# Two channels per position in the exchanged tile, and the first chunk's taps on TensorE

## The chip, the cores and the metric

The kernel runs on one NeuronCore of one Trainium2 chip. The metric is device time in microseconds (us) of one execution. All operands are float32. The engines are TensorE (PE; its weight loads are listed apart as PEld), VectorE (DVE), ScalarE (ACT), GpSimd (POOL) and SyncE (SP), which issues nearly all DMAs. Each engine takes its instructions in the order of the program.

## What is computed

The sequence has 2,048 positions, the model 512 channels. The reference, cut to what matters:

```python
# A: short causal convolution of k (4 taps per channel), times v,
#    then a causal convolution of 2,048 taps per channel, done with FFTs
k_shift = sum(k_pad[:, t:t + S, :] * shift_k[:, ks - 1 - t] for t in range(ks))
kv = k_shift * v
y = irfft(rfft(kv, 2 * S) * rfft(ssm_k, 2 * S))[:S] + kv * ssm_D
a = q * y
# B: two tokens of the 2,048 are chosen by a score and go through a SwiGLU FFN
r = x @ w_r                                  # x is q
idx = argsort(-r)[:2]
upd = (silu(x[idx] @ w_gate) * (x[idx] @ w_up)) @ w_down * sigmoid(r[idx])
b = x; b[idx] += upd
g = sigmoid((x * gate_w).sum(-1))
out = g * a + (1 - g) * b                    # = q * (g * y + (1 - g)), plus two rows
```

## The kernel before

The 512 channels are worked in four chunks of 128 (`c` = 0 to 3). The long convolution is done with Fourier transforms written as matrix products: a transform of 2,048 is split into one of 64 and one of 32, with a change of layout between them. Each chunk goes through these steps, which are named generators in the code; `c` is the chunk, the other index a part of it:

- `taps(c, x)`, x = 0 to 3: the four taps of k on a quarter of the positions, channels on partitions. ScalarE scales the first shifted window of `kT` into `acc` (line 167). For chunk 0 VectorE adds the other three (line 171, `TAPS_DVE`); for chunks 1 to 3 ScalarE scales each into `tap` (line 174) and GpSimd adds it (line 176).
- `T(c, x)`: TensorE transposes `acc` in four blocks of 128 x 128 into PSUM (line 185), and VectorE multiplies the result by v into the chunk's `kv` tile (line 187).
- `A(c, b)`, b = 0 to 3: the transform of 64 of the long filter `hN` (line 158). Before it `D(t)` (`skip`, lines 138 to 142) adds the row `drow` to the filter's first tap on GpSimd.
- `C(c, b)`: the same transform of `kv` (line 199). It needs all four T of the chunk.
- `exchange` (line 149), once for each A and each C, eight times a chunk: VectorE transposes 32 x 32 blocks of the PSUM result, 128 x 1024, into the tile `e`, where now the 32 inner positions lie on the partitions. `e` is laid out [channel group, position k, 4 channels].
- `S(c, u)`, u = 0 to 7: the transform of 32 of both, filter and kv, for four positions k each (line 212): 16 matmuls that run on tiles of 64 rows x 32 columns of the array. The moving operand is `e[r, :, k, :]`, 64 groups (two halves of 32) of 4 channels. It needs all eight exchanges of the chunk. ScalarE copies one factor out of PSUM (`g`, line 217), VectorE forms the two products of spectra (lines 222, 223), and GpSimd their sums (line 229).
- `I(c, u)`: the inverse transform of 32 (line 241), copied by ScalarE into `f` (line 246). `f` is laid out [channel pair, position, 2 channels].
- `X(c, i)`: VectorE transposes 32 x 32 blocks of `f` in place (line 254).
- `J(c, mb)`: the inverse transform of 64 (line 263), whose moving operand is `f[:, :, k, :]`, 64 groups of 2 channels; the gate g*y + (1-g) on ScalarE (line 271; on VectorE, line 273, for two blocks of the last chunk), the product with q on GpSimd (line 276; VectorE for those two), and the store.
- `G` (`ffn`): router, choice of the two tokens and FFN, cut into about thirty pieces, on TensorE with small steps on VectorE. `Z(c)` adds the update of the two rows to chunk c's output by an indirect DMA on GpSimd's queue (line 401).

Loads are steps too: `Lk` (`kT`), `Lv` (v), `Lh` (the filter), `Lq` (q), `Lw` (q transposed for the router, then the FFN's weights: the tile `wff`) take the next piece of a stream, `L0` to `L11` the constants (`w1`, `w2`, `w3`, `vv` are the transforms' matrices, `ident` the identity, `shk` the taps). All are issued on SP, in order; a load into a buffer in use waits there, and what stands behind it waits too. `kT` has two buffers of two parts each, v three buffers, `hN` and `wff` two each, q four.

The order of everything is written out by hand, in the string `ORDER`: each word advances that generator to its next `yield`, and what it issues there stands in each engine's program in that order. No planner changes it. PSUM is divided by hand as well: pool `ps2` has three buffers, used by A, C, S, I and the last chunk's J; pool `ps` has one, for T and the other J; pool `psf` one, for G.

Of the kernel before, what the change touches and what calls it, by code (L numbers as in the profile page):

```python
# [8 lines left out]
F32 = mybir.dt.float32  # L9
# [7 lines left out]
S, D, F = 2048, 512, 1792  # L17
NC, DC = 4, 128
# [5 lines left out]
TAPS_DVE = {(0, 0), (0, 1), (0, 2), (0, 3)}  # L24
# [7 lines left out]
L5 L3 Lk L0 Lk L8 taps0.0 taps0.1 taps0.0 taps0.0 Lk taps0.0 Lk Lv L2 Lv taps0.1 taps0.1 taps0.2 L1 L4 taps0.1 L9  # L32
taps0.2 Lh taps0.2 taps0.3 D0 Lw T0.1 Lh Lk Lw T0.1 taps0.3 D1 T0.0 L10 T0.0 A0.0 Lv taps0.3 taps0.3 Lv A0.1 A0.2
taps0.2 A0.2 T0.3 A0.0 Lv taps1.0 taps1.0 T0.3 G taps1.0 A0.3 Lk Lh Lk T0.2 A0.3 taps1.0 Lw Lw T0.2 Lh C0.0 A0.1
C0.0 C0.1 C0.2 C0.3 Lv Lk taps1.1 taps1.1 taps1.2 D2 L6 G C0.1 Lw taps1.1 C0.3 taps1.2 C0.2 taps1.1 taps1.2 A1.1
A1.0 A1.1 A1.0 T1.0 S0.2 taps1.3 T1.0 S0.0 Lw taps1.2 S0.2 S0.1 taps1.3 D3 Lk S0.2 T1.1 Lk G S0.0 taps1.3 S0.1 S0.0
taps1.3 S0.1 S0.1 L7 A1.2 taps2.1 S0.3 A1.2 Lv taps2.1 S0.3 Lv Lw S0.5 Lw T1.1 S0.5 I0.0 taps2.1 T1.3 G S0.5 S0.3
S0.3 S0.4 T1.3 S0.4 S0.4 I0.0 S0.6 I0.0 T1.2 Lh taps2.1 S0.5 Lq Lw T1.2 G A1.3 D4 I0.1 taps2.0 A1.3 S0.6 taps2.0 G
Lv I0.1 S0.6 C1.0 T2.1 Lv C1.0 Lk G I0.1 Lw C1.2 C1.2 C1.1 taps2.0 Lh C1.1 S0.7 taps2.2 taps2.0 taps2.2 G Lk S0.7
C1.3 C1.3 S0.7 T2.1 I0.2 A2.1 G taps2.2 taps2.2 S1.2 Lv T2.0 I0.2 I0.2 A2.1 G S0.7 I0.3 taps2.3 T2.0 taps2.3 G S1.2  # L40
T2.2 S1.0 S1.2 Lk I0.3 I0.3 S1.0 S1.0 S1.1 taps2.3 taps2.3 S1.1 S1.3 S1.1 S1.1 S1.3 G T2.2 S1.4 taps3.0 taps3.0 S1.4
S1.3 G Lk I1.0 L11 D5 S1.4 G G A2.0 Lw Lw I1.0 I1.0 taps3.1 Lv A2.3 X0.1 A2.0 T2.3 S1.3 S1.5 Lq A2.3 X0.0 S1.7 G
S1.5 Lv taps3.0 G Lq S1.5 S1.5 taps3.0 X0.3 S1.7 Lw I1.1 I1.2 Lw I1.1 I1.1 Lk T2.3 X0.2 C2.3 C2.3 S1.7 J0.0 J0.0 G
taps3.1 I1.2 G J0.0 taps3.1 Lh I1.2 taps3.1 J0.1 C2.1 A2.2 Lw Lw Lq C2.1 J0.1 C2.0 J0.1 C2.2 C2.0 A2.2 C2.2 Lh
taps3.2 G G Lk J0.2 J0.2 S1.6 S2.1 Lw Lw S2.0 J0.3 S1.6 G D6 G S1.6 taps3.2 J0.2 S2.1 S2.1 Lv A3.0 Lv Lw S2.0 S2.0
S1.7 A3.1 A3.1 J0.3 taps3.2 I1.3 T3.1 J0.0 A3.0 D7 taps3.3 Lw T3.1 taps3.2 I1.3 I1.3 S2.1 S2.3 taps3.3 Lv X1.2 S2.3
S2.2 T3.2 S2.3 T3.2 G X1.1 Lw G S2.2 A3.3 I2.0 taps3.3 taps3.3 I2.0 I2.0 T3.3 A3.3 T3.3 J0.3 S2.6 Lq S2.2 S2.7 X1.0
T3.0 S2.3 S2.7 G S2.7 Lw J0.2 G I2.1 Lw A3.2 S2.6 S2.6 T3.0 I2.1 I2.1 X1.3 S2.5 S2.5 S2.5 S2.4 J0.1 J1.2 A3.2 S2.4
S2.7 Lw G G C3.0 C3.0 I2.3 Lq S2.4 G I2.3 I2.3 C3.1 C3.3 C3.2 C3.1 C3.3 Lw S2.5 J1.2 I2.2 Lw C3.2 Lq J1.0 J0.3 J1.2
Lq I2.2 I2.2 J1.0 S3.0 S3.0 X2.0 J1.0 S3.1 S3.7 S3.1 X2.2 J1.1 S3.0 J1.1 J1.1 J1.2 S3.1 Lq X2.1 S3.7 G Lw S3.6 S3.7  # L50
S3.6 S3.6 S3.2 S3.1 S3.2 Lw J1.3 X2.3 I3.0 J1.1 S3.7 S3.2 J1.0 J1.3 Lq J1.3 S3.3 S3.3 S3.3 S3.3 G J2.2 J2.2 Lq S3.5
# [468 lines left out]
```

## Time and profile before

| | |
|---|---|
| median of 3 runs | 198.1 us (197.37 to 198.25) |
| the profiled execution | 198.09 us, of which 196.1 us are the span shown by the profile |
| TensorE busy | 146.9 us (75%) |
| TensorE weight loads busy | 70.3 us (36%) |
| VectorE busy | 150.6 us (77%) |
| ScalarE busy | 93.3 us (48%) |
| GpSimd busy | 115.4 us (59%) |
| DMA | 39.77 MB, mean 203 GB/s |

A group in the profile has the line, the engine, the operation, the output and its inputs by name, partitions x elements, and the count; then busy time in us and the mean length of one in ns; then the idle time of the engine just before these instructions and what ended it. In the order of time a row begins with its start and its length in us, and merges neighbours. A row of waits names who waited, for whom, the total in us, how many times, and the longest. A row of a window has its bounds and length, then the busy time (and count) of TensorE, its weight loads, VectorE, ScalarE and GpSimd, the granted TensorE clock, the busy share of the DMA engines, and GB/s. The trace lists each float32 matmul as two records of matmul and two of weight load; a transpose on TensorE is one.

### The profile page before, as it was taken

To read this page: it belongs to the slowest core of one execution; us is meant where nothing else is said; L and a number is where in the kernel's file an instruction comes from. 1 tells how busy PE (TensorE), PEld (TensorE's weight loads), DVE (VectorE), ACT (ScalarE), POOL (GpSimd) and SP (SyncE) were. 2 spreads that over 40 slices of the span, in tenths; PEclk is the share of its full clock that TensorE was granted. 3 is DMA by queue.
4 is the path that set the end of the run, shared out by engine and by line. 5 is a ranking of instruction groups with operands and counts; after the bars stand their busy time and mean duration, and the time that the engine had idled before them with its cause. 6 is when DMAs were issued, how large, how long until landed. Compare 5 with 4: busy or idle time off the path is not lost. (4 is left out here: it accounts for less than half of the span.)

```text
span 196.1 us, 4562 instructions
## 1 busy us (share of the span) xinstructions
PE 146.9 (75%) x1822; PEld 70.3 (36%) x1822; DVE 150.6 (77%) x179; ACT 93.3 (48%) x178; POOL 115.4 (59%) x107
## 2 busy tenths in 40 slices
PE   0028748788978797998897999899989997974700
PEld 0014222334523234542443534444356452423600
DVE  0198799997889998999769879988999845047540
ACT  0611655265597245753395672432556555660500
POOL 0021889159899276974595898460613992931662
PEclk9999999999999999999999999999999999998885
DMA  5999994858699300079578464675640757786140
GB/s 133 366 324 273 341 341 166 295 196 310 210 322 349 119 0 4 3 246 336 194 271 278 159 230 142 208 232 174 187 149 24 261 140 242 184 275 209 60 159 0
DMA packets 16473, 39.77 MB, mean 203 GB/s; under 512 B 2361, under 2 KB 2883, under 8 KB 16325
## 3 DMA queue, kind: packets, MB, share of 16 engines
q1 hardware_dynamic: 16292, 39.48, 60.7%
q8 instruction: 14, 0.23, 0.5%
q0 software_dynamic: 160, 0.01, 0.2%
q14 instruction: 7, 0.05, 0.1%
HBM read 35.28 MB, written 4.20 MB: 201 GB/s over the span
## 5 line engine op out<-in xcount | busy, mean ns | idle before, releaser
L149 DVE STREAM_TRANSPOSE e<-p 128x1024 f32<-128x1024 f32 x32 | 62.8, 2041 | 5.6 <-PE p L199 2.9
L229 POOL TENSOR_TENSOR y<-y 128x512 f32<-128x512 f32 x32 | 40.3, 1282 | 21.6 <-DVE y L222 21.3
L176 POOL TENSOR_TENSOR acc<-acc,tap 128x512 f32<-128x512 f32 x36 | 45.9, 1280 | 11.1 <-ACT tap L174 6.7
L212 PE MATMUL p<-e,w 64*32 64x256 f32 x1024 | 32.7, 380 | 5.9 <-DVE e L149 5.1
L241 PE MATMUL p<-y,w 64*128 64x512 f32 x128 | 31.8, 611 | 3.2 <-POOL y L229 1.4
L246 ACT ACTIVATE f<-p 128x512 f32<-128x512 f32 x32 | 18.1, 625 | 25.2 <-PE p L241 25.1
L276 POOL TENSOR_TENSOR qN<-oA,qN 128x512 f32<-128x512 f32 x14 | 17.9, 1278 | 20.3 <-ACT oA L271 16.2
L217 ACT ACTIVATE g<-p 128x512 f32<-128x512 f32 x32 | 18.9, 598 | 22.5 <-PE p L212 15.0
L222 DVE TENSOR_TENSOR y<-p,g 128x512 f32<-128x512 f32 x32 | 21.8, 682 | 9.3 <-PE p L241 4.1
L174 ACT ACTIVATE tap<-kT,shk 128x512 f32<-128x512 f32 x36 | 25.4, 718 | 4.3 <-POOL acc L176 4.1
L212 PEld LDWEIGHTS p<-e,w 64*32 64x32 f32 x1024 | 17.7, 106 | 19.8 <-DVE e L149 8.5
L254 DVE STREAM_TRANSPOSE f<-f 128x1024 f32<-128x1024 f32 x16 | 19.3, 1223 | 7.0 <-ACT f L246 7.0
L185 PE MATMUL ps<-ident,acc 128*128 128x128 f32 x64 | 11.4, 305 | 16.1 <-DVE acc L171 13.5
L271 ACT ACTIVATE oA<-ps,omg,gcol 128x128 f32<-128x128 f32 x48 | 18.0, 460 | 11.4 <-PE ps L263 9.1
L223 DVE TENSOR_TENSOR y<-p,g 128x512 f32<-128x512 f32 x32 | 21.8, 683 | 1.0 <-POOL y L229 0.7
L199 PE MATMUL p<-kv,w 64*128 64x512 f32 x64 | 17.3, 640 | 5.1 <-DVE e L149 2.1
L158 PE MATMUL p<-hN,w 64*128 64x512 f32 x64 | 18.0, 661 | 1.8 <-DVE e L149 1.2
L241 PEld LDWEIGHTS p<-y,w 64*128 64x128 f32 x128 | 11.5, 186 | 18.4 <-issue 9.3
L185 PEld LDWEIGHTS ps<-ident,acc 128*128 128x128 f32 x64 | 7.3, 150 | 25.6 <-DVE acc L171 13.5
L167 ACT ACTIVATE acc<-kT,shk 128x512 f32<-128x512 f32 x16 | 11.2, 719 | 10.9 <-DMA kT<-in_kT_dram 10.8
L171 DVE SCALAR_TENSOR_TENSOR acc<-kT,shk,acc 128x512 f32<-128x512 f32 x12 | 8.7, 748 | 9.1 <-ACT acc L167 8.9
L140 POOL TENSOR_TENSOR hN<-hN,drow 1x32 f32<-1x32 f32 x16 | 5.2, 324 | 15.0 <-DMA hN<-in_hN_dram 14.4
(63 smaller groups left out, 117.0 us busy)
## 6 DMA issues: line engine op xcount, KB each, us to landing
vN<-in_vN_dram SPq DMA_DIRECT2D x16, 256.0 KB, 5.2
hN<-in_hN_dram SPq DMA_DIRECT2D x8, 512.0 KB, 5.3
wff<-in_qT_dram SPq DMA_DIRECT2D x8, 512.0 KB, 5.6
qN<-in_qN_dram SPq DMA_DIRECT2D x16, 256.0 KB, 3.4
out_dram<-qN SPq DMA_DIRECT2D x16, 256.0 KB, 3.8
wff<-in_wg_dram SPq DMA_DIRECT2D x8, 448.0 KB, 4.1
wff<-in_wu_dram SPq DMA_DIRECT2D x8, 448.0 KB, 4.6
wff<-in_wd_dram SPq DMA_DIRECT2D x8, 448.0 KB, 5.6
```

Of the source, the lines that this page charges most:

```text
L149: nc.vector.transpose(ee[c][:, i, b * 8:(b + 1) * 8].rearrange("p d k e -> p d e k"), p)
L174: nc.scalar.activation(s, w[j], AF.Copy, scale=shk[:, c, j:j + 1])
L176: nc.gpsimd.tensor_add(acc, acc, s)
L185: nc.tensor.transpose(p[:, i], acc[:, i * 128:(i + 1) * 128], ident)
L212: nc.tensor.matmul(p[32 * j:32 * j + 32, b, ri].rearrange("p i d -> p (i d)"), w2[r, 4 * u + j, 32 * ri:32 * ri + 32], e[r, :, 4 * u + j, ...
L217: nc.scalar.activation(g, p[:, :, :, 0], AF.Copy)
L222: nc.vector.tensor_mul(y1[:, u % 2], p[:, :, :, 1], g)
L223: nc.vector.tensor_mul(y2[:, u % 2], p[:, :, ::-1, 1], g)
L229: nc.gpsimd.tensor_tensor(w[:, :, 0], w[:, :, 0], w[:, :, 1], op=op)
L241: nc.tensor.matmul(p[:, j], w3[r, w], y[r, :, ri], start=(n == 0), stop=(n == len(parts) - 1))
L246: nc.scalar.activation(ff[c][:, :, o:o + 4].rearrange("p d k e -> p k d e"), p[:, j].rearrange("p k (d e) -> p k d e", e=2), AF.Copy)
L254: nc.vector.transpose(w, w)
```

## The change

There are three parts.

First, the tile `e` keeps two channels side by side instead of four. It has the same size; an exchange writes 16 groups of two where it wrote 8 groups of four, and S reads its moving operand as 128 groups of 2 channels.

Second, chunk 0 (`TAPS[0] = "PPPP"`) has no `taps` steps any more. In T the tap sum and the transpose are one series of matmuls: the shifted window of `kT`, 64 channels x 128 positions, is the weight, and a diagonal matrix of 64 x 64 that holds one tap of these channels (`dg`, a new constant prepared on the host) is the moving operand. For each of four blocks of positions, four taps are added up in PSUM, for the two halves of the channels apart: 32 matmuls for a T, into a buffer of `ps2`, the halves in two banks. VectorE multiplies by v in two pieces of 64 channels. Chunks 1 to 3 keep their taps on ScalarE and GpSimd (`A`).

Third, `ORDER` is rewritten throughout. `L1` is now `dg`, and the constants behind it count one higher (`L2` is `ident`, `L6` and `L7` are `w2`). `kT` and `dg` are loaded first; the four T of chunk 0 stand first on TensorE, then the four C, then the four A; two A of chunk 1 that stood ahead of the first S now stand behind the fourth.

```diff
-TAPS_DVE = {(0, 0), (0, 1), (0, 2), (0, 3)}
+TAPS = ["PPPP", "AAAA", "AAAA", "AAAA"]
+NPE = 1
...
 ORDER = """
-L5 L3 Lk L0 Lk L8 taps0.0 taps0.1 taps0.0 taps0.0 Lk taps0.0 Lk Lv L2 Lv taps0.1 taps0.1 taps0.2 L1 L4 taps0.1 L9
-taps0.2 Lh taps0.2 taps0.3 D0 Lw T0.1 Lh Lk Lw T0.1 taps0.3 D1 T0.0 L10 T0.0 A0.0 Lv taps0.3 taps0.3 Lv A0.1 A0.2
...
+Lk L1 Lk Lv L0 L9 T0.0 T0.0 Lk Lk L4 T0.1 Lv Lv Lw T0.2 T0.2 T0.1 L3 Lv Lk T0.3 T0.3 C0.2 Lk C0.1 Lw C0.3 C0.2
+taps1.0 Lh taps1.0 G Lk taps1.0 L5 D0 taps1.0 C0.0 taps1.1 C0.1 C0.3 Lh D1 L2 C0.0 taps1.1 A0.1 A0.0 A0.1 A0.0 A0.3
+Lk Lw Lw A0.3 A0.2 L6 T1.0 taps1.1 L11 A0.2 L7 G taps1.2 S0.0 taps1.1 taps1.2 S0.0 S0.0 taps1.2 Lh taps1.2 Lw Lw Lv
...
+    dg = const.tile([128, NPE, 4, 64], F32, name="dg")
...
-            ee[c] = epool.tile([128, 2, DC // 4, 32, 4], F32, name="e")
+            ee[c] = epool.tile([128, 2, DC // 2, 32, 2], F32, name="e")
         mark(("e", c))
-        nc.vector.transpose(ee[c][:, i, b * 8:(b + 1) * 8].rearrange("p d k e -> p d e k"), p)
+        nc.vector.transpose(ee[c][:, i, b * 16:(b + 1) * 16].rearrange("p d k e -> p d e k"), p)
...
-            if (c, x) in TAPS_DVE:
+            if TAPS[c][x] == "D":
...
+        to = kvs[c][:, :, 4 * x:4 * x + 4, :]
+        v = vst.get(4 * c + x)
+        if TAPS[c][x] == "P":
+
+            kt = kst.get(4 * c + x)
+            o = 512 * (x % 2) + 192
+            p = ps2.tile([128, 2, 4, 2, 64], F32, name="p2")
+            for i in range(4):
+                for j in range(4):
+                    for h in range(2):
+                        r = slice(64 * h, 64 * h + 64)
+                        w = o + 128 * i - 64 * j
+                        nc.tensor.matmul(p[:, h, i, 0], kt[r, w:w + 128], dg[r, c, j], start=(j == 0), stop=(j == 3),
+                                         skip_group_check=True)
+            yield
+            for h in range(2):
+                nc.vector.tensor_mul(to[:, 32 * h:32 * h + 32].rearrange("p d m e -> p m d e"),
+                                     p[:, h, :, 0].rearrange("p m (d e) -> p m d e", e=2),
+                                     v[:, :, 64 * h:64 * h + 64].rearrange("p m (d e) -> p m d e", e=2))
+        else:
+            acc = accs.pop((c, x))
...
-            for f in (A, C, I, J, T, X, taps):
+            for f in (A, C, I, J, T, X) + (() if TAPS[c][u] == "P" else (taps,)):
...
+    z = A_shift_k.reshape(NC, 2, 64, 4)[:NPE]
+    dg = np.zeros((2, 64, NPE, 4, 64), np.float32)
+    i = np.arange(64)
+    dg[:, i, :, :, i] = z.transpose(2, 1, 0, 3)
+    r["dg"] = dg.reshape(128, NPE, 4, 64)
```

In the changed kernel the exchange is line 150, the new matmuls are line 195, their products line 199, C's matmuls line 219, S's line 232.

More of the change, by code (lines that the diff above doesn't have):

```diff
@@ L37 @@
[L37 to L51, printed above, removed]
```

41 lines of the change are left out of this document (26 added, 15 removed).

## The prediction

> **What bounds the kernel now.** I read the busy shares first, then the span cut into three stages, the groups of instructions, TensorE's waits inside the middle stage, and last the order of time at both ends. The cuts are where the first block of step S starts on TensorE (37.03 us) and where the last one ends (161.3 us):
>
> ```profile
> 0.00:37.03 37.03, 17.58 (x76) 6.76 (x76) 26.19 (x25) 13.29 (x19) 15.97 (x22) 1.00 0.82 273
> 37.03:161.30 124.27, 110.20 (x1594) 53.16 (x1594) 110.91 (x135) 67.67 (x130) 83.24 (x73) 1.00 0.58 192
> 161.30:196.10 34.80, 19.10 (x162) 10.42 (x154) 13.53 (x20) 12.35 (x30) 16.23 (x13) 0.86 0.52 164
> ```
>
> After each length come the busy times of TensorE, its weight loads, VectorE, ScalarE and GpSimd. In the 124.27 us of the middle TensorE works 110.20 and VectorE 110.91: two engines that run in program order and wait for each other by turns. The first stage is VectorE's and the loads' (26.19 against TensorE's 17.58); the third is a chain in which no engine is full.
>
> ```profile
> L149 DVE STREAM_TRANSPOSE e<-p 128x1024 f32<-128x1024 f32 x32 | 62.8, 2041 | 5.6 <-PE p L199 2.9 <-PE p L158 2.7
> L149 DVE STREAM_TRANSPOSE e<-p 128x1024 f32<-128x1024 f32 x24 | 47.6, 2044 | 4.4 <-PE p L199 2.9 <-PE p L158 1.5
> L254 DVE STREAM_TRANSPOSE f<-f 128x1024 f32<-128x1024 f32 x16 | 19.3, 1223 | 7.0 <-ACT f L246 7.0
> L171 DVE SCALAR_TENSOR_TENSOR acc<-kT,shk,acc 128x512 f32<-128x512 f32 x12 | 8.7, 748 | 9.1 <-ACT acc L167 8.9
> L187 DVE TENSOR_TENSOR kv<-ps,vN 128x512 f32<-128x512 f32 x16 | 10.9, 683 | 0.6 <-PE ps L185 0.6
> L222 DVE TENSOR_TENSOR y<-p,g 128x512 f32<-128x512 f32 x32 | 21.8, 682 | 9.3 <-PE p L241 4.1 <-ACT g L217 3.9 <-POOL acc L176 0.8
> L352 DVE COPY xsT<-pf 128x128 f32<-128x128 f32 x1 | 0.3, 292 | 0.0
> PE p L212 <- DVE e L149: 5.1, 6, 1.6
> PE p L199 <- DVE e L149: 1.4, 2, 1.0
> PE p L241 <- DVE e L149: 0.8, 2, 0.5
> ```
>
> The exchange transposes (line 149) are VectorE's largest group: 62.8 us, 1.96 each, 24 of them in the middle stage (second row). The last three rows are TensorE's waits for them there: 7.3 of its 14.1 us of idle time (124.27 - 110.20).
>
> **The transposes.** Line 149 writes four channels side by side, so that successive elements of its output lie 16 bytes apart; after the change they lie 8 apart. Line 254 transposes as many elements and both reads and writes at 8 bytes: 1.21 each (19.3 / 16). Bounds are 1.96 (no gain) and 1.0 (its 1,024 elements at the slope between the last two VectorE rows, (682 - 292) ns / 384 elements = 1.02 ns, with nothing fixed). I take 1.21, the row with the same write. That saves 0.75 x 32 = 24 us of VectorE, 18 of them in the middle, whose VectorE work falls from 111 to 93.
>
> What the write gains, step S could lose when it reads: its moving operand now comes in runs of two elements, 256 bytes apart, instead of four.
>
> ```profile
> 95.28 1.11 PE L263 MATMUL ps<-f,vv 128*64 128x128 f32 x16
> 37.03 1.10 PE L212 MATMUL p<-e,w 64*32 64x256 f32 x32
> 145.93 2.83 PE L212 MATMUL p<-e,w 64*32 64x256 f32 x96 [0.65 <-DVE e L149]
> ```
>
> Step J (line 263) reads its operand in exactly such runs: 8 rounds of 128 columns in 1.11 us. A block of S, 4 rounds of 256, takes 1.10, and three in a row 2.83. Equal columns, equal time: I charge nothing. Were it not so, TensorE would pay 3.2 us for each 0.1 us per block.
>
> **Chunk 0's taps.** Gone: four scalings on ScalarE (off the path), twelve accumulations on VectorE (8.7 us), 16 transposes on TensorE. New: four steps T0.x of 32 matmuls, each 64 rows by 128 weights with 64 columns moving. The trace counts an f32 matmul as two records, so a step has 64 weight loads, 32 on each half of the rows.
>
> ```profile
> 78.31 1.15 PE L349 MATMUL pf<-ident,pe 2*128 2x128 f32 x8
> L349 PE MATMUL pf<-ident,pe 2*128 2x128 f32 x8 | 1.2, 283 | 0.0
> 70.40 0.66 PE L185 MATMUL ps<-ident,acc 128*128 128x128 f32 x4
> 22.84 0.30 PEld L158 LDWEIGHTS p<-hN,w 64*128 64x128 f32 x4 [1.54 <-DVE e L149]
> 22.84 1.13 PE L158 MATMUL p<-hN,w 64*128 64x512 f32 x4 [0.63 <-DVE e L149]
> L158 PE MATMUL p<-hN,w 64*128 64x512 f32 x64 | 18.0, 661 | 1.8 <-DVE e L149 1.2 <-issue 0.6
> ```
>
> Eight records with 128 weights and 128 columns each (L349) take 1.15 us: less 0.28, the whole length of one, that is 0.124 for each of the others; the transposes of line 185 go at (0.66 - 0.28) / 3 = 0.13. Two halves side by side: block A has four weight loads on two halves, done in 0.30 where four in a row would take 0.5, and its four products carry 2,048 columns in the time in which J carries 1,024. So a step costs 32 x 0.125 = 4.0, all four 16.3 with the drain. Bounds: 64 columns at 0.92 ns (2.83 us for three blocks of S, 1,024 columns each) are 59 ns a pair, 1.9 us a step, if the weights hide entirely; 8.0 a step if the halves take turns. I take 4.0, since the two rows have the same 128 weights. VectorE multiplies each step's result in two pieces of 256 elements, 292 + 128 x 1.02 = 0.42 each; over the chunk 3.4 against 4 x 0.68.
>
> **The first stage after.** The old start and its loads:
>
> ```profile
> 0.74 0.38 SPq L121 DMA_DIRECT2D w<-in_w_dram  x1
> 1.95 0.43 SPq L121 DMA_DIRECT2D shk<-in_shk_dram  x1
> 6.82 1.28 ACT L167 ACT_TABLE_LOAD   x1 [6.82 <-DMA shk<-in_shk_dram]
> 8.87 6.01 DVE L171 SCALAR_TENSOR_TENSOR acc<-kT,shk,acc 128x512 f32<-128x512 f32 x8 [8.87 <-ACT acc L167]
> 13.49 1.12 PE L185 MATMUL ps<-ident,acc 128*128 128x128 f32 x4 [13.49 <-DVE acc L171]
> 20.69 3.96 DVE L149 STREAM_TRANSPOSE e<-p 128x1024 f32<-128x1024 f32 x2 [1.20 <-PE p L158]
> hN<-in_hN_dram SPq DMA_DIRECT2D x8, 512.0 KB, 5.3
> w<-in_w_dram SPq DMA_DIRECT2D x2, 512.0 KB, 5.5
> ```
>
> TensorE stood until 13.49 behind ScalarE and VectorE. Now kT is the first load and dg the second (1.2 us); at the 4.9 us that shk took (6.82 - 1.95) T0.0 starts at 6.2 and T0.3 ends at 22.5. Its products take VectorE until 23.4, the first block of C 1.13 more (as A's), then come eight exchanges of 1.21: S could start at 34.2. In the old order A's exchanges ran from 20.7 on; now C and A both stand behind T0 on TensorE. On SP's queue the reloads of kT's two buffers wait for T0.1 (14.3) and T0.3 (22.5), and behind them stand h(0), then the second row of drow, h(1) and ident. h(1), issued by 24, lands at 29.5 with the 5.3 of its row, and its skip on GpSimd is done by 30.2; the seventh exchange needs it at about 30.6. The first half of w2 stands behind two wff tiles that wait for the first router product, behind the third C block (27.5): issued 28.5, landed 34 by its row, later by up to 2 with 1 MB ahead of it. I take 35.5 (37.03 before). Bounds: 31 if steps are short and w2 comes early, 50 if the halves take turns.
>
> **The middle stage after.** Between the first and the last block of S the program's order on TensorE holds the same groups as before and two blocks of A more (A1's, before S0 until now): 110.2 + 2 x 1.1 (18.0 / 16) = 112.4. To it comes idle time. The 7.3 us behind exchanges should go, since VectorE is then busy for 93 us and not 111; the other 6.8 are waits for sums, for gates and for the router's small VectorE steps. All of them kept: 119.2. All gone: 112.4. TensorE's share of 94% in the last quarter, quoted here, says the same as the first:
>
> ```profile
> 130.00:161.30 31.30, 29.41 (x484) 14.95 (x480) 26.37 (x29) 15.55 (x35) 16.60 (x14) 1.00 0.54 169
> PE p L241 <- POOL y L229: 1.4, 3, 0.5
> ```
>
> I take 118: some of the router's and the sums' waits shrink with a VectorE that is less behind. GpSimd has 83 us there and ScalarE 68, and neither gains.
>
> **The tail.** The order after the last S holds what it held: three I, three J, two down products, the update, then J3.
>
> ```profile
> 173.26 1.50 ACT L271 ACTIVATE oA<-ps,omg,gcol 128x128 f32<-128x128 f32 x4
> 176.19 1.02 PE L396 MATMUL pf<-pe,sel 128*2 128x512 f32 x2 [0.79 <-DVE pe L393]
> 176.05 3.49 DVE L254 STREAM_TRANSPOSE f<-f 128x1024 f32<-128x1024 f32 x3
> 179.46 0.70 DVE L398 TENSOR_SCALAR pe<-pf,fac 2x512 f32<-2x512 f32 x1
> 179.69 5.26 PE L263 MATMUL p<-f,vv 128*64 128x128 f32 x64 [2.48 <-DVE f L254]
> 192.07 1.58 POOLq L514
> ```
>
> From ScalarE's last f (173.26) to J3 it took 6.4 us. Now the update's scaling stands on VectorE ahead of the last two X transposes: gate 1.5, J2 1.1, the update's matmul 1.0, scaling 0.7, two transposes 2.4, and 0.3 for the handovers, an estimate from the gaps of the rows: 7.0. So 34.8 becomes 35.3. From J3 on nothing changes.
>
> **Sum.** 35.5 + 118 + 35.3 = 188.8 us of span. The profiled execution took 198.09 for 196.1, 2.0 around it: 190.8. It agrees with the median of 198.1; 0.5% of that, about 1 us, is what can be told from no change.
>
> **Rivals.**
> (a) The T0 steps cost 2 to 3 us and TensorE runs on almost without idle time: 32 + 113 + 35 + 2 = 182. For it: the moving side needs only 1.9; against: the rows with 128 weights.
> (b) A half loads new weights only when its previous product has streamed: 0.125 + 0.06 a record, 128 x 0.185 = 23.7, S at 42, 197. Against: line 185's transposes, 128 weights and 128 columns on all rows, would then take 0.245 each and take 0.13. [...]
> (c) The halves take turns: 8.0 a step, T0 ends at 38.5, S starts at 50, and the time is 50 + 118 + 35.3 + 2 = 205: slower. The place is the four T0 steps alone; it decides from a step of 6 us on, where the 7.3 us that I expect to gain are used up. Against: A's loads and products.
> (d) The exchange keeps 1.96, because reading PSUM and not the write sets it; line 254 reads SBUF. Then the eight exchanges end at 40.2 and the middle stays at 124 and more: 40.2 + 125 + 35.3 + 2 = 202. Against: line 222 reads PSUM at 1.0 ns an element and line 149 takes 1.9. [...]
> (e) TensorE's idle time only moves, to waits for GpSimd's sums and the three PSUM buffers that T0 now shares: the middle stays near 125, 198 in all. For it: both engines idle 11% today though neither is full.
>
> **Chances.** Forecast (185 to 196.5) 0.58, (a) 0.14, (b) 0.06, (c) 0.10, (d) 0.05, (e) 0.07. Faster: forecast, (a) and a third of (b) and (e): 0.76. Same 0.07, slower 0.17 with (c), (d) and the rest. The range takes (a), (b) and (e) in, up to the lower end of (d), and leaves (c) out: 180.5 to 200.
>
> **What will show it.** Line 150 (the exchange) at about 1.2 us; line 232 (S) still 1.1 a block; line 195's steps of about 4 us from 6 us on; S starting at 35.5; TensorE at 95% of the middle and VectorE under 80%. The forecast fails if T0 takes over 6 us a step, if S waits for w2 beyond 38, or if the middle keeps TensorE's share at 89%.

## The result, and the profile after

The changed kernel takes 229.4 us (median of 4 runs, 227.46 to 231.48) against 197.7 us for the kernel before beside it: a ratio of 1.157, 95% interval 1.148 to 1.165. It is 16% slower, where 4% faster was forecast, and the time lies far outside the forecast range. The profiled execution has a span of 225.5 us. Medians are of all runs; ratios and intervals leave out executions in a slower state, as the profiled ones of the old order, of T0 on whole rows, of the moved loads and of the warm start were.

The three stages of the changed kernel, cut as in the prediction at the first and the last block of S on TensorE; columns as there (window, length, busy time of TensorE, weight loads, VectorE, ScalarE, GpSimd, granted clock, DMA share, GB/s):

```profile
0.00:46.90 46.90, 40.46 (x308) 31.94 (x309) 12.46 (x16) 8.79 (x12) 11.38 (x16) 1.00 0.55 176
46.90:193.80 146.90, 125.29 (x1602) 57.51 (x1602) 96.03 (x135) 72.30 (x135) 86.60 (x78) 0.92 0.55 186
193.80:225.50 31.70, 17.61 (x160) 9.92 (x154) 13.80 (x20) 11.41 (x28) 17.30 (x14) 0.85 0.42 136
```

Against the forecast of 35.5, 118 and 35.3 us the start is 11.4 us longer, the middle 28.9 us longer and the tail 3.6 us shorter. VectorE got the relief that was promised: 96.0 us of the middle where it had 110.9. But TensorE works 125.3 us there (forecast 112.4) and stands idle for 21.6 (146.90 - 125.29; forecast 5.6).

Groups of the changed kernel, by line (instructions, then busy us and mean ns of one, then idle time before them):

```profile
L150 DVE STREAM_TRANSPOSE e<-p 128x1024 f32<-128x1024 f32 x32 | 38.6, 1237 | 13.5 <-PE p L159 8.3 <-PE p L219 5.2
L195 PE MATMUL p<-dg,kT 64*128 64x64 f32 x256 | 27.6, 418 | 4.2 <-DMA dg<-in_dg_dram 4.2
L232 PE MATMUL p<-e,w 64*32 64x256 f32 x1024 | 40.4, 455 | 1.3 <-DMA w<-in_w_dram 1.3
```

The exchange costs 38.6 / 32 = 1.21 us, as forecast. A T0 step costs 27.6 / 4 = 6.9 us, not 4.0. S's matmuls take 455 ns each where they were to be unchanged; in the order of time the same shows block by block, and beside it two of TensorE's long waits:

```profile
4.22 27.57 PE L195 MATMUL p<-dg,kT 64*128 64x64 f32 x256 [4.22 <-DMA dg<-in_dg_dram]
32.69 5.49 PE L219 MATMUL p<-kv,w 64*128 64x512 f32 x12 [0.90 <-PE p L195]
39.21 1.17 PE L219 MATMUL p<-kv,w 64*128 64x512 f32 x4
87.77 0.98 PE L393 MATMUL pf<-wff,xsT 128*32 128x224 f32 x8 [4.52 <-DMA wff<-in_wg_dram]
88.68 3.79 PE L261 MATMUL p<-y,w 64*128 64x512 f32 x8
93.25 3.67 PE L232 MATMUL p<-e,w 64*32 64x256 f32 x96
103.41 2.09 PE L393 MATMUL pf<-wff,xsT 128*32 128x224 f32 x16 [6.49 <-DMA wff<-in_wg_dram]
108.27 1.99 PE L261 MATMUL p<-y,w 64*128 64x512 f32 x8
```

Three blocks of S in a row take 3.67 us; they took 2.83. The three C blocks right behind T0 take 5.49 us, 1.8 each, and the next one 1.17: TensorE is slow during T0 (6.9 us a step) and in the 5.49 us behind it. And the feed-forward matmuls (line 393) wait for their weights; the two I blocks behind the first such gap take 3.79 where two usually take 1.99, at a granted clock of 0.50 over them.

Who waits for whom, in total us, times and the longest: TensorE in the middle stage, then the DMA queue of SP over the whole span.

```profile
PE pf L393 <- DMA wff<-in_wg_dram: 11.0, 2, 6.5
PE pf L393 <- DMA wff<-in_wu_dram: 7.7, 4, 6.0
SPq L87 <- DVE kv L208: 54.6, 8, 15.5
```

18.7 of TensorE's 21.6 us of idle time are waits for wff tiles. On the queue that issues those loads (SPq) the largest wait is for line 208, VectorE's product of a tap sum with v, which frees a buffer of vN. One such place in the order of time on SP's queue of the changed kernel:

```profile
67.55 0.38 SPq L87 DMA_DIRECT2D wff<-in_wg_dram  x1
83.50 0.33 SPq L87 DMA_DIRECT2D vN<-in_vN_dram  x1
83.92 0.38 SPq L87 DMA_DIRECT2D wff<-in_wg_dram  x1
```

For 15.6 us SP issues nothing: a vN load waits for its buffer, and the wff load behind it in the written order goes out right after it, at 83.92. It lands at 87.77, when line 393 starts.

So there are three suspects: S's reads, T0's step, and the loads behind vN. My theory at this point was that each costs its own part and the parts add; the rivals for each are told with the runs.

### The profile page after: what moved, and what is told of

It is laid out like the page before. It is cut to its first block, busy times and chain, and to the rows that moved or that the text cites. A ratio compares the mean times of both kernels' runs of the same rounds, so it can differ in the third digit from the quotient of the medians.

```text
span 225.5 us, 5017 instructions
## 1 busy us (share of the span) xinstructions
PE 183.3 (81%) x2062; PEld 99.4 (44%) x2062; DVE 122.3 (54%) x171; ACT 92.5 (41%) x174; POOL 115.3 (51%) x107
## 5 line engine op out<-in xcount | busy, mean ns | idle before, releaser
L249 POOL TENSOR_TENSOR y<-y 128x512 f32<-128x512 f32 x32 | 41.1, 1309 | 10.6 <-DVE y L242 6.0
L150 DVE STREAM_TRANSPOSE e<-p 128x1024 f32<-128x1024 f32 x32 | 38.6, 1237 | 13.5 <-PE p L159 8.3
L232 PE MATMUL p<-e,w 64*32 64x256 f32 x1024 | 40.4, 455 | 1.3 <-DMA w<-in_w_dram 1.3
L261 PE MATMUL p<-y,w 64*128 64x512 f32 x128 | 34.5, 663 | 0.0
L195 PE MATMUL p<-dg,kT 64*128 64x64 f32 x256 | 27.6, 418 | 4.2 <-DMA dg<-in_dg_dram 4.2
L195 PEld LDWEIGHTS p<-dg,kT 64*128 64x128 f32 x256 | 27.4, 330 | 4.2 <-DMA kT<-in_kT_dram 4.2
L393 PE MATMUL pf<-wff,xsT 128*32 128x224 f32 x128 | 10.7, 430 | 19.0 <-DMA wff<-in_wg_dram 11.0
L291 ACT ACTIVATE oA<-ps,omg,gcol 128x128 f32<-128x128 f32 x48 | 18.1, 464 | 11.6 <-PE ps L283 8.8
L219 PE MATMUL p<-kv,w 64*128 64x512 f32 x64 | 19.8, 716 | 0.9 <-PE p L195 0.9
L199 DVE TENSOR_TENSOR kv<-p,vN 128x256 f32<-128x256 f32 x8 | 2.9, 418 | 29.7 <-PE p L195 29.7
L159 PE MATMUL p<-hN,w 64*128 64x512 f32 x64 | 16.5, 608 | 0.0
L283 PEld LDWEIGHTS ps<-f,vv 128*64 128x64 f32 x192 | 11.0, 141 | 9.1 <-ACT f L266 2.4
(65 smaller groups left out, 121.3 us busy)
```

The source lines that it names most:

```text
L150: nc.vector.transpose(ee[c][:, i, b * 16:(b + 1) * 16].rearrange("p d k e -> p d e k"), p)
L195: nc.tensor.matmul(p[:, h, i, 0], kt[r, w:w + 128], dg[r, c, j], start=(j == 0), stop=(j == 3), skip_group_check=True)
L219: nc.tensor.matmul(p[:, par].rearrange("p (d e) m -> p d e m", e=2), w1[r], x[r], start=True, stop=True)
L232: nc.tensor.matmul(p[32 * j:32 * j + 32, b, ri].rearrange("p i d -> p (i d)"), w2[r, 4 * u + j, 32 * ri:32 * ri + 32], e[r, :, 4 * u + j, ...
L249: nc.gpsimd.tensor_tensor(w[:, :, 0], w[:, :, 0], w[:, :, 1], op=op)
L261: nc.tensor.matmul(p[:, j], w3[r, w], y[r, :, ri], start=(n == 0), stop=(n == len(parts) - 1))
```

## The experiments

### The layout alone, and the changed kernel without it

The first kernel is the one before with nothing but the new layout of `e`; the second is the changed kernel with the old layout.

```diff
-            ee[c] = epool.tile([128, 2, DC // 4, 32, 4], F32, name="e")
+            ee[c] = epool.tile([128, 2, DC // 2, 32, 2], F32, name="e")
...
-        nc.vector.transpose(ee[c][:, i, b * 8:(b + 1) * 8].rearrange("p d k e -> p d e k"), p)
+        nc.vector.transpose(ee[c][:, i, b * 16:(b + 1) * 16].rearrange("p d k e -> p d e k"), p)
```

> The kernel before with one part alone: two channels per position in e, old order, old taps. Theory P (three causes that add up: T0's weight loads pass one at a time, 0.107 us for each 128 columns; blocks of S take 1.24 instead of 0.94 us because they read pairs; and the new order lets the FFN's weights stand on SP's queue behind loads of v that wait): exchanges 1.2 us, blocks of S 1.24, TensorE work of the middle stage up by 32 x 0.3 = 9.6 us to 120, VectorE's down by 18: 196 to 203 us. Rival R1 (S is slower after the change because of a lower TensorE clock or the order, not because of pairs): S stays at 0.94 and the time falls to 185 to 190.

> The changed kernel with four channels per position again; T0 on TensorE and the new order stay. P: blocks of S back to 0.94, exchanges 1.96, the first eight of them cost 6 us more; the waits on SP's queue stay: 220 to 230 us. R1: S stays at 1.2 and above, exchanges slower: 232 to 240.

The layout alone gives 186.8 us (185.74 to 187.32; ratio 0.939, 0.930 to 0.947). The changed kernel with the old layout takes 240.4 (ratio 1.207, 1.196 to 1.218). The layout is a gain of some 11 to 13 us in either kernel; the loss comes from the rest. Neither theory came whole in either run: S goes to 452 ns with the layout and is back at 2.83 us for three blocks without it, as the first has it, but the first had the time 9 us too high here and 10 too low there, and both times lie at or near the second's range. The first two stages of the layout alone, and its S:

```profile
0.00:33.40 33.40, 17.72 (x76) 7.33 (x76) 21.45 (x25) 13.31 (x19) 14.08 (x20) 1.00 0.86 292
33.40:151.20 117.80, 115.66 (x1593) 54.02 (x1592) 97.29 (x135) 70.41 (x131) 87.79 (x76) 1.00 0.62 209
L212 PE MATMUL p<-e,w 64*32 64x256 f32 x1024 | 40.7, 452 | 0.2 <-DVE y L223 0.2
```

The middle is 117.8 us, the 118 that I forecast, but for another reason than mine: TensorE's idle time falls to 2.1 us, further than I dared, and its work rises from 110.2 to 115.7, because S's matmuls went to 452 ns. Their group in the profile of before:

```profile
L212 PE MATMUL p<-e,w 64*32 64x256 f32 x1024 | 32.7, 380 | 5.9 <-DVE e L149 5.1
```

From 32.7 to 40.7 us is 8 us more of TensorE, against 23.5 us less of VectorE (62.8 - 39.3).

### The new T0 in the old order

The changed kernel with the order of before: the `taps0` words dropped, the load of `dg` put behind the first kT.

```diff
-L5 L3 Lk L0 Lk L8 taps0.0 taps0.1 taps0.0 taps0.0 Lk taps0.0 Lk Lv L2 Lv taps0.1 taps0.1 taps0.2 L1 L4 taps0.1 L9
+L5 L3 Lk L12 L0 Lk L8 Lk Lk Lv L2 Lv L1 L4 L9 Lh D0 Lw T0.1 Lh Lk Lw T0.1 D1 T0.0 L10 T0.0 A0.0 Lv Lv A0.1 A0.2 A0.2
```

> The changed kernel (T0 on TensorE by halves, two channels per position) with the order of the kernel before: the taps of chunk 0 left out of it and dg loaded behind the first kT. Theory O (the rewritten order is the largest cause): T0 27 us in all stays, S starts at 36 to 42, and the time is 190 to 199. Rival (the order is innocent; T0 on TensorE, which holds kT's buffers longer and starts chunk 1's taps late, is the cause): 212 to 229.

209.6 us (207.13 to 215.61; ratio 1.048, 1.038 to 1.058). By ratios on about 199 us, the layout gives -0.061 (12 us), the new T0 then +0.109 (22 us), the new order another +0.109 (22 us), the parts taken in this sequence; the time lies in neither of the two expected ranges. The same records run at different speeds here, and three windows inside T0 show at what granted clock (the value right behind the five busy times):

```profile
7.77 13.92 PE L195 MATMUL p<-dg,kT 64*128 64x64 f32 x128 [7.77 <-DMA kT<-in_kT_dram]
27.67 5.93 PE L195 MATMUL p<-dg,kT 64*128 64x64 f32 x64 [1.36 <-DVE e L150]
37.27 6.93 PE L195 MATMUL p<-dg,kT 64*128 64x64 f32 x64
27.60:30.00 2.40, 2.33 (x34) 2.33 (x34) 1.15 (x2) 1.05 (x2) 2.32 (x2) 0.79 0.96 377
30.00:32.00 2.00, 2.00 (x22) 2.00 (x21) 0.00 (x0) 1.52 (x3) 1.19 (x2) 0.50 0.03 10
40.00:44.20 4.20, 4.20 (x40) 4.01 (x38) 0.00 (x0) 0.00 (x0) 0.00 (x0) 0.50 0.00 0
```

34 records in 2.33 us are 0.069 us each at a mean clock of 0.79; 40 in 4.20 are 0.105 each at 0.50. The third step begins fast, behind blocks of A and 1.36 us of idle time, and falls to half clock while it runs (second window). The DMA engines are 0.96 busy in the first window and idle in the other two (0.03 and 0.00), so it is not the loads that hold T0 back.

### One step varied at a time: the patterns of T0 and of S

In one kernel, each of the four T0 steps and each chunk's S reads or multiplies in another pattern.

```diff
+            if x == 0:    # as it was: halves alternate
+            elif x == 1:  # all 64 records on one half of the rows
+            elif x == 2:  # the tap is the outermost loop
+            else:         # whole rows, 128 x 128 moving, 16 matmuls
...
+                    if c == 0 and u < 4:    e[r, :, 4 * u + j, :]      # tiles 8 bytes apart
+                    elif c == 0:            e[r, :, 4 * u, :]          # all four tiles the same pairs
+                    elif c == 1:            (g k e)[:, :, 4 * u + j, :], k=32, e=4
+                    elif c == 2 and u < 4:  flat[(4 * u + j) * 256:][:256]
+                    elif c == 2:            (g k)[:, :, 4 * u + j], k=32
+                    elif u < 4:             (g k e)[:, 4 * (u % 4) + j, 0:2], k=16, e=4   # tiles 16 bytes apart
+                    else:                   (g k e)[:, j % 2, :], k=2, e=2
```

> The changed kernel with other access patterns, for the length of single steps (the values it computes from them are not those of the reference). T0.0 as it is. T0.1: all 64 loads on one half of the rows. T0.2: the tap outermost, so that successive matmuls add to other PSUM columns. T0.3: whole rows, 32 loads of 128 columns with 128 columns moving. P: 6.85, 6.85, 6.85 and 3.4 to 4.1 us. Rival R2 (a half loads new weights only when its own previous product is through, 0.214 each): 6.85, 13.7, 6.85, 6.9. Rival R3 (successive matmuls that add to the same PSUM columns wait for each other): 6.85, 6.85, 2 to 4, 3.5 or more. Blocks of S: chunk 0 u<4 as it is 1.24; chunk 0 u>=4 all four column tiles read the same pairs; chunk 1 runs of four 0.94; chunk 2 u<4 one run of 256: 0.94; chunk 2 u>=4 single elements 128 bytes apart: 1.9 or more if each run costs, 0.94 if not; chunk 3 u<4 pairs 256 bytes apart: 1.24; chunk 3 u>=4 pairs 16 bytes apart: 1.24 if the run's length decides, 0.94 if the distance does. The whole time is no test: 200 to 240.

T0's four steps in the order of time, and five of S's patterns by group:

```profile
4.34 7.09 PE L195 MATMUL p<-dg,kT 64*128 64x64 f32 x64 [4.34 <-DMA dg<-in_dg_dram]
11.20 13.64 PE L202 MATMUL p<-dg,kT 64*128 64x64 f32 x63
24.70 7.18 PE L208 MATMUL p<-dg,kT 64*128 64x64 f32 x63
31.81 5.71 PE L213 MATMUL p<-dg,kT 128*128 128x128 f32 x32
L252 PE MATMUL p<-e,w 64*32 64x256 f32 x128 | 5.2, 451 | 1.0 <-DMA w<-in_w_dram 0.9
L256 PE MATMUL p<-e,w 64*32 64x256 f32 x128 | 8.8, 643 | 0.8 <-DVE y L287 0.8
L272 PE MATMUL p<-e,w 64*32 64x256 f32 x128 | 3.9, 377 | 0.2 <-DVE y L287 0.2
L268 PE MATMUL p<-e,w 64*32 64x256 f32 x128 | 11.4, 875 | 0.0
L276 PE MATMUL p<-e,w 64*32 64x256 f32 x128 | 4.9, 392 | 0.1
```

On S: the changed kernel's pattern takes 451 ns (L252). The same runs of two, 256 bytes apart, take 377 ns when the four column tiles that work at the same time read 16 bytes apart (L272), as fast as the old runs of four. When all four tiles read the very same pairs it is 643 ns (L256). So at this step of 256 bytes neither the run of two nor the step costs anything by itself: what costs is that column tiles read inside the same 16 bytes at the same time (451 against 377).

That is not a rule for every step. Pairs that follow each other at 16 bytes (L276) take 392 ns, although all four tiles read inside the same 16 bytes there. Single elements 128 bytes apart, the four tiles side by side (L268), take 875; this kernel does not separate the tiles' sharing from the single elements. Why sharing costs at the wide step (451) and hardly at the narrow one (392) stays open.

On T0: the order of the taps does nothing (7.18). All 64 records on one half take 13.64 us, 0.213 each, against 0.107 when the halves alternate: the halves do work side by side, and rival (c) of the prediction, that they take turns, is out as a mechanism, though its price is near. Why 0.107 and not 0.0625 is answered below, by the clock.

### S's column tiles spread, 64 bytes apart

The layout alone, with S's four column tiles on groups 8j + u instead of 4u + j (tiles 64 bytes apart); the constants `w2` and `vv` are reordered on the host to fit.

```diff
-                                     w2[r, 4 * u + j, 32 * ri:32 * ri + 32], e[r, :, 4 * u + j, :],
+                                     w2[r, 4 * u + j, 32 * ri:32 * ri + 32], e[r, :, 8 * j + u, :],
```

> layout_only with one more edit: the four column tiles of a block of S take positions 8 apart (8j + u) instead of neighbours (4u + j), with the constants permuted to match, so that no two tiles read the same 16 bytes at once. Theory L (two column tiles that read within one 16-byte line wait for each other; the length of the run does not matter): blocks of S 0.94 us again, TensorE 32 x 0.3 = 9.6 us less work, 177 to 182 us. Rival R (pairs cost as such): 1.24 and 186 to 188.

182.6 us (181.88 to 183.3; ratio 0.917, 0.910 to 0.924): the fastest kernel of the study, 4.2 us below the layout alone. Its middle stage and S:

```profile
32.50:146.30 113.80, 109.23 (x1595) 53.51 (x1596) 94.70 (x134) 67.54 (x131) 85.75 (x76) 1.00 0.64 213
L212 PE MATMUL p<-e,w 64*32 64x256 f32 x1024 | 31.7, 378 | 0.4 <-DVE y L223 0.4
```

S is back at 378 ns. TensorE's work in the middle falls by 6.4 us and the stage by 4.0 (117.8 to 113.8).

### T0 on whole rows

The changed kernel with T0 on all 128 rows: a 128 x 128 diagonal, 16 matmuls of 128 weights and 128 columns a step, one product on VectorE. The diagonal stands in the tile of `vv`, a constant that is loaded late, and so has that name in the profile.

```diff
...
-                for j in range(4):
-                    for h in range(2):
...
+                    nc.tensor.matmul(p[:, 0, i].rearrange("p a b -> p (a b)"), kt[:, w:w + 128], dg[:, j],
+                                     start=(j == 0), stop=(j == 3), skip_group_check=True)
```

> The changed kernel with T0's matmuls over whole rows: a diagonal of 128 x 128 moves, half as many weight loads, one product of 512 elements on VectorE. P: T0 3.4 to 4.1 us a step, S starts at 35 to 38 instead of 46.9, and the time is 216 to 221; if the waits on SP's queue came only from the late start, 205 to 212. R2: T0 stays at 6.85 a step and the time at 229.

219.9 us (217.15 to 223.1; ratio 1.096, 1.084 to 1.109): 0.060 less than the changed kernel, some 12 us. T0 takes 17.40 us and S starts at 36.0 instead of 46.9:

```profile
L193 PE MATMUL p<-vv,kT 128*128 128x128 f32 x128 | 17.4, 307 | 4.4 <-DMA vv<-in_dg_dram 4.4
```

A second kernel varied T0 again, to tell the weights' load from the columns: halves with 128 columns moving, whole rows with 64, halves with 256, whole rows with 128.

```diff
+            if x == 0:    # halves, 128 columns moving
+            elif x == 1:  # whole rows, 64 columns
+            elif x == 2:  # halves, 256 columns
+            else:         # whole rows, 128 columns
```

> The changed kernel with other shapes in T0, for the length of single steps (the values are not those of the reference). T0.0: halves, 128 columns moving instead of 64. T0.1: whole rows, 64 columns moving, 20 matmuls. T0.2: halves, 256 columns moving. T0.3: whole rows, 128 columns moving, 16 matmuls with other data. Theory H1 (a half's next weights take 0.213 after the last ones, whatever streams): T0.0 6.85, T0.2 6.85 to 7.7. Theory H2 (a half loads only when its product is through: 0.107 + columns x 0.83 ns + 0.053): T0.0 8.5, T0.2 12. For whole rows: 0.134 a record would give T0.1 5.4 and T0.3 4.3; 0.213 a record 8.5 and 6.8.

The first, the third and the last of these steps on TensorE:

```profile
4.15 6.40 PE L195 MATMUL p<-dg,kT 64*128 64x128 f32 x64 [4.15 <-DMA dg<-in_dg_dram]
15.09 7.18 PE L209 MATMUL p<-kT 64*128 64x256 f32 x64
22.20 3.84 PE L214 MATMUL p<-dg,kT 128*128 128x128 f32 x32
```

Halves with 128 columns took 6.40 us for 64 records, no more than with 64 columns in the same place (7.09 in the first of these kernels); halves with 256 columns 7.2; whole rows 0.112 to 0.117 a record, with 64 columns as with 128. So between 64 and 128 columns the columns do not set the pace. That the load of the weights does, as the prediction had it, agrees with a window of T0 on whole rows in which TensorE's weight loads are busy throughout (4.00 of the 4.00 us from 13.00 on), but no run varied that load by itself. What this leaves open is why a record of half the rows costs as much as one of all rows, though two halves run side by side: the first step and the others did not run at the same clock, as the next run shows.

### Dense products beside T0: the clock

What fits all of it is the clock that the windows of the old order show. To test that, two of the changed kernel's T0 steps get dense products that nobody reads (all rows, 512 columns): six ahead of T0.1, one ahead of each quarter of T0.3.

```diff
...
+                for n in range(6):
+                    nc.tensor.matmul(d.rearrange("p a b -> p (a b)"), kt[:, 128:256], kt[:, 0:512], start=True, stop=True, skip_group_check=True)
```

> The changed kernel with dense products on TensorE that nobody reads (all 128 rows, 128 weights, 512 columns, two records each) beside two of the four T0 steps: six ahead of T0.1's 64 records, and one ahead of each of the four output groups of T0.3. T0.0 and T0.2 stay as they are. Theory of the clock: the T0 steps took 6.85 us because TensorE ran at half clock, which records of 64 rows and 64 columns do not raise; at full clock their step costs 3.4 us. Then T0.0 still takes 6.85; the first six dense products begin at 0.8 to 0.9 us a record pair and a half and speed up to about 0.95 us a product; T0.1's 64 records behind them take 3.4 to 4.5 us, T0.2 begins at that rate and slows, and T0.3 takes about 3.4 + 4 x 0.95 = 7.2. Rival: a T0 record costs 0.107 us at any clock (its weights are loaded one by one). Then T0.1's 64 records take 6.85 as before, T0.2 6.85, and T0.3 6.85 + 3.8 = 10.6. In both the later stages move back by the dense products, and the time is 225 to 240.

TensorE of this kernel in the order of time (start and length in us; L202 and L220 are the dense products, L198, L208, L216 and L225 the four T0 steps):

```profile
4.12 7.09 PE L198 MATMUL p<-dg,kT 64*128 64x64 f32 x64 [4.12 <-DMA dg<-in_dg_dram]
11.14 7.87 PE L202 MATMUL ps<-kT 128*128 128x512 f32 x12
18.94 3.79 PE L208 MATMUL p<-dg,kT 64*128 64x64 f32 x64
22.57 3.74 PE L216 MATMUL p<-dg,kT 64*128 64x64 f32 x64
26.23 1.13 PE L220 MATMUL ps<-kT 128*128 128x512 f32 x2
27.29 1.11 PE L225 MATMUL p<-dg,kT 64*128 64x64 f32 x16
```

The same 64 records take 7.09 us ahead of the dense products and 3.79 behind them. The first dense products are slow too: the first six of their twelve records start 0.7 to 1.0 us apart, the others 0.43. The trace keeps the changes of the granted clock with their times, and its first entry is a rise to full at 16.1 us, 5.0 us after the first dense product; ahead of that first entry the views print 1.00 although nothing is recorded there. The clock theory holds: at full clock a pair of half records costs 0.117 us (3.74 / 32), about what a whole-row record costs (0.114, below), and 0.21 at half clock (2 x 0.105, in the old order's window at 0.50). That T0's price is the same at any clock is out. The kernel as a whole takes 228.6 us, no less than the changed one: the dense products cost what they save, and the middle has its other faults. Two things of the theory did not come: T0.2 was to slow down again, and it ran its 3.74 us at the full rate; and T0.3 with its dense products took 8.5 us, not 7.2 (10.6 by the rival).

The clock entries of the other traces agree. In the changed kernel the first is a rise at 38.4 us, behind T0 and the three slow blocks of C; in the old order a rise at 25.6 and a fall at 29.0, 1.3 us into the third step. The kernel with T0 on whole rows rises at 10.5: in the 6.0 us before, 28 records start, 0.215 us each, the price of two half records at half clock; the other 100 take 11.4 us, 0.114 each. At the same clock, then, whole rows cost what a pair of halves costs, and that kernel gained because the clock rose 6.0 us after its matmuls began. Nor is it the number of rows that decides: with the halves of 128 columns moving (6.40 us above) it rose 5.4 us after their start, and with those of 64 columns it did not in 27.57.

With dense products the rise came after 5.0 us here and after 3.2 in the warm start below. It did not come with every activity: 256 records of 64 rows and 64 columns, back to back for 27.57 us, passed without one.

### The loads behind vN

The changed kernel with seven words of its order moved: seven loads of vN go behind the wff loads that followed them (two of the seven are in the line shown).

```diff
-A1.3 I0.1 I0.1 S0.7 D4 Lw C1.0 Lv Lw I0.1 T2.1 C1.0 taps2.2 Lq Lv G Lk G Lh D5 I0.3 T2.0 T2.0 I0.3 I0.3 S1.0 taps2.3
...
+A1.3 I0.1 I0.1 S0.7 D4 Lw C1.0 Lw Lv I0.1 T2.1 C1.0 taps2.2 Lq G Lk G Lh D5 I0.3 T2.0 T2.0 I0.3 I0.3 S1.0 taps2.3
...
```

> The changed kernel with seven loads of v moved behind the loads of the FFN's weights that follow them in the order; nothing else moved. Theory O': TensorE's 18.7 us of waits for wff come from loads of v that wait on SP's queue, and they bring the lowered clock with them: 203 to 214 us. Rival (the weights' buffers or the late taps hold it anyway): 222 to 230.

208.3 us (205.51 to 209.27; ratio 1.036, 1.024 to 1.047): 21 us less by the medians, 0.121 or some 24 us by the ratios, for seven words, as the theory has it. The middle stage and TensorE's wait for wff in it:

```profile
46.20:175.00 128.80, 121.27 (x1600) 56.49 (x1600) 97.70 (x135) 71.90 (x135) 87.03 (x78) 0.96 0.62 212
PE pf L393 <- DMA wff<-in_wg_dram: 3.6, 2, 3.1
```

The second largest wait, for the wu half of the wff tiles, is gone, and the stage falls by 18.1 us, from 146.9 to 128.8. TensorE's idle time in it gives 14.1 of them (21.6 to 7.5) and its work 4.0 (125.3 to 121.3), at a granted clock of 0.96 instead of 0.92: the speed behind the gaps, 0.50 over the two I blocks above, had been part of the cost.

### Putting the parts together

Two kernels repair all three faults. The first: moved loads, T0 on whole rows, spread tiles. The second has the same loads and tiles but keeps T0 in halves as the change wrote it, and lets TensorE multiply zeros in three dense products while it waits for kT and dg:

```diff
+    zz = vv[:, 0:10].rearrange("p a b -> p (a b)")
+    nc.vector.memset(zz, 0.0)
+    d0 = ps.tile([128, 4, DC], F32, name="ps")
+    for n in range(3):
+        nc.tensor.matmul(d0.rearrange("p a b -> p (a b)"), zz[:, 0:128], zz[:, 128:640], start=True, stop=True,
+                         skip_group_check=True)
```

> The changed kernel with all three repairs: the seven loads of v behind the FFN's weights (as in after_lw), T0 over whole rows (as in after_k128), and S's column tiles 8 apart (as in spread). If the three costs add up, 229 less 21 (after_lw), less 10 (after_k128), less 4 to 9 (spread against layout_only, and 32 x 0.3): 188 to 195 us. If a late T0 was what made the order bad, the repairs overlap: 198 to 206.

> The changed kernel with three repairs at once: the seven loads of vN moved as in the run with the moved loads, S's column tiles spread over the lines as in the run with spread tiles, and a warm start: VectorE writes zeros to 640 columns of a constant's tile that is loaded late, and TensorE multiplies them in three dense products (128 rows, 128 weights, 512 columns, never read) while it would wait for kT and dg. If the half clock made the T0 steps long, the three products take 2.0 us each at half clock and end at 7 us, T0 runs from there at 3.75 us a step and ends at 22 to 23 (forecast 22.5, measured 31.8), S starts at 35.5 to 38, and with -9 us from T0 and -4 from S against the 208.3 us of the run with moved loads the time is 192 to 197. If the zeros do not raise the clock or the early idle time counts for nothing, T0 stays at 27 us, ends at 34, and the time is 204 to 208.

The first takes 195.1 us (194.69 to 196.61; ratio 0.985, 0.976 to 0.993). The second takes 196.2 against 199.8 beside it; its four runs lie from 191.25 to 197.88, all below the seven of before (198.33 to 201.22), too scattered for an interval. Its start, TensorE in the order of time, and its stages:

```profile
1.59 4.40 PE L120 MATMUL ps<-vv 128*128 128x512 f32 x6 [1.59 <-DVE vv L117]
5.92 14.51 PE L201 MATMUL p<-dg,kT 64*128 64x64 f32 x256
35.45 2.84 PE L238 MATMUL p<-e,w 64*32 64x256 f32 x96 [0.83 <-DMA w<-in_w_dram]
0.00:35.45 35.45, 32.11 (x314) 21.39 (x315) 13.15 (x17) 8.41 (x12) 9.19 (x15) 0.95 0.72 237
35.45:163.25 127.80, 115.25 (x1600) 56.77 (x1601) 95.63 (x135) 71.06 (x136) 87.65 (x80) 0.96 0.63 213
163.25:195.90 32.65, 19.32 (x156) 11.54 (x154) 13.14 (x20) 11.65 (x28) 17.10 (x14) 0.79 0.43 134
```

And the load of the first half of w2 on SP's queue there:

```profile
28.13 0.42 SPq L128 DMA_DIRECT2D w<-in_w_dram  x1
```

T0 takes 14.51 us, 3.6 a step, S starts at 35.45 and its three blocks take 2.84. The first stage is the forecast's, 35.5 us, and the tail is 2.7 us better than forecast; the middle stays 9.8 us over.

A last one puts whole-row T0 and the spread tiles into the old order, against the fastest kernel, which has the old taps there; T0 adds up in the single buffer of pool `ps` here, so that a step can have to wait for VectorE's product of the one before (1.1 us in all):

```diff
-L5 L3 Lk L0 Lk L8 taps0.0 taps0.1 taps0.0 taps0.0 Lk taps0.0 Lk Lv L2 Lv taps0.1 taps0.1 taps0.2 L1 L4 taps0.1 L9
+L5 L3 Lk L12 L0 Lk L8 Lk Lk Lv L2 Lv L1 L4 L9 Lh D0 Lw T0.1 Lh Lk Lw T0.1 D1 T0.0 L10 T0.0 A0.0 Lv Lv A0.1 A0.2 A0.2
```

> Old order, two channels per position, column tiles of S 8 apart, and chunk 0's taps on TensorE over whole rows (4.3 us a step as in after_k128, one product on VectorE). If the taps on TensorE are worth having in the old order: 3 to 6 us below spread, 173 to 179. If TensorE is the bound already and they only add to it: 180 to 186.

199.2 us (197.97 to 201.92; ratio 0.999, 0.994 to 1.004), 17 us behind the old taps and above both expected ranges. S starts at 41.4 us instead of 32.5, the middle takes 120.0 instead of 113.8, and TensorE has 161.4 us of work where it had 145.6. Summing taps on TensorE costs the fullest engine 15.8 us and takes some 9 us off VectorE, which with the new layout has only 129 of 180 us to do. Even in the order written for it this T0 gave 195.1.

## Why the prediction was wrong, point by point

**The exchange: right.** 1.21 us a transpose (38.6 / 32), the row with the same write step. Rival (d) is out.

**S charged nothing: wrong, by its own price.** "Equal columns, equal time" took J's row as proof. J reads its operand in runs of two, but its two column tiles read 128 bytes apart (positions k and k + 16), where S's neighbours k = 4u + j now share 16 bytes; the spread run shows that this, not the run, costs here. Of three blocks in a row each takes 1.22 us (3.67 / 3) instead of 0.94 (2.83 / 3); at the 3.2 us for each 0.1 that the prediction named, that is 9.0 us of TensorE over the kernel, and 9.0 is what the groups of the layout alone and of the spread tiles differ by (40.7 and 31.7). In time, spreading them gave 4.2 us.

**T0's step: the rows were right, the clock was not.** 4.0 us a step is what it costs at full clock (3.6 to 3.8 measured); at the start of this kernel a record took 0.107 us (6.9 / 64), the price at a granted clock of 0.50 in the old order (0.105), and 27.57 us of these small matmuls brought no rise (the first is at 38.4 us): 6.9 a step, 27.6 in all instead of 16.3. The failing step is the choice of rows "since the two rows have the same 128 weights": both came from the middle of the kernel, at full clock. The sign stood in the prediction's own fences: the four transposes of line 185 that take 0.66 us at 70.40 took 1.12 at 13.49, where the profile shows a clock of 1.00 as well; the first clock entry of that trace is the rise at 19.0 us. The forecast's condition, "fails if T0 takes over 6 us a step", was met; rival (c) came near that price (8.0) by another mechanism.

**The first stage: right in its chain, wrong by T0.** It came out at 46.9. With T0 at full clock, S started at 35.45, and the load of the first half of w2 went out at 28.13, where 28.5 was worked out.

**The middle: the step that failed is that I did not walk SP's queue there.** I argued only from TensorE's and VectorE's old idle time, "the other 6.8 are waits for sums, for gates and for the router's small VectorE steps". The new order puts seven vN loads, each waiting for a buffer, ahead of wff loads: 18.7 us of waits on TensorE that no row of before could show, but that the text of the two orders did. Moving the seven loads took 15.1 of them away. Rival (e), "idle time only moves", named the effect, with GpSimd and the PSUM buffers as its place and 7 us as its price (125 for 118); the place was the load queue, and the idle time 16 us over the forecast. The other 12.9 us are TensorE's work, 125.3 instead of 112.4: 9.0 are S's, and the rest goes with the granted clock of 0.92. The gain that was expected came in full: TensorE's waits for the exchange are gone from the middle.

**The tail: 31.7 instead of 35.3.** I had the tail 0.5 us longer than before; it is 3.1 shorter. The layout alone has 33.4 (184.6 - 151.2), which is 1.4 of them; no run takes the rest apart.

**Summed up.** Over 190.8 - 2.0 = 188.8 of span the profiled 225.5 is 36.7 us: start +11.4 (clock), middle +28.9 (16 idle, 9 S's reads, the rest a lower clock), tail -3.6. By the ratios, on 199 us, the runs gave back 24 us for the loads, 12 for T0 and, measured in the old order, 4 for S's tiles: 40, where the first repaired kernel gained 34 (1.157 to 0.985). So the parts nearly add up, some 6 us short.

**Open.** Even so repaired, the middle takes 127.8 us in the new order (126.1 with T0 on whole rows) and 113.8 in the old one with the same S. Of the 14.0 between, 4.8 are a wait for wff that remains, and 6.0 are more work on TensorE: 2.2 for the two blocks of A that stand in the middle only in the new order, and the rest at a clock of 0.96. Which entries of the order cause the other idle time was not tried.

## What to carry to other kernels

Take the price of a TensorE instruction from a row at the same place in the kernel, not only of the same shape: in these kernels T0's record took 0.107 us at the start and 0.058 behind the first rise of the clock, which came 5.0 us after dense products began beside T0, and three products of zeros during the wait for the first load took T0 from 27.6 us to 14.5. When an order is rewritten, walk each DMA queue in it: one load that waited for a buffer held back the loads written behind it, for 15.6 us at one place of the changed kernel. And when a layout changes, look at what all the tiles that read at the same time touch, not only at the pattern of one.

## What the runs showed of the hardware

- Column tiles of TensorE that streamed at the same time, each in pairs 256 bytes apart, took longer when they read inside the same 16 bytes: 451 ns a matmul for two pairs in 16 bytes, 643 when four tiles read the same pairs, 377 when they read 16 bytes apart, 378 at 64 bytes apart. With pairs 16 bytes apart, four tiles inside the same 16 bytes cost hardly anything (392).
- Matmuls of 64 rows, 128 weights and 64 columns did not raise the clock: 27.57 us of them passed without a gap and without a rise, and in the old order the clock fell from full to 0.50 in a step of them that began behind 1.36 us of idle time. With 128 columns moving the same halves saw the rise 5.4 us after their start, and whole rows with 128 columns after 6.0. At full clock the records of 64 columns ran on at full rate for the 7.5 us of two steps (warm) and the 14.51 us of four (warm start); what decides between these cases stays open.
- Three dense products whose operands are all zeros were enough for a rise: in the warm start it is recorded 3.2 us after the first of them begins.
- Ahead of the first recorded rise a whole-row record of 128 weights took 0.215 us and a record of half the rows, with the halves by turns, 0.107 (0.105 where the windows show a clock of 0.50); behind it, 0.114 and 0.058.
- The clock shown by the profile reads 1.00 from the start in kernels whose first matmuls take twice as long as the same ones later (7.09 us and 3.79 for 64 records in warm). In the changed kernel the first entry of the trace is the rise at 38.4 us, and what the views show before it is not recorded.
